# Eight transposes in a step, turned values, later loads, and blocks of unread 512-column products in an attention and feed-forward kernel

## The chip, the core and the metric

The kernel runs on one core of a Trainium2 chip. The metric is the device time of one execution in microseconds (us). The core's engines are named as the profile names them: PE (TensorE, the products; PEld is its weight load), DVE (VectorE), ACT (ScalarE), POOL (GpSimd) and SP (SyncE, which here only issues DMAs). They run side by side, each in its own order, and wait for each other by semaphores.

## The reference

Eight batches, eight heads, 512 local and 32 global tokens, 64 values a head. Attention comes first: global tokens look at everything, a local token looks at the global ones and at local ones no more than 32 away. Its output is the input of a feed-forward layer that mixes each token with the one before it. The core of both, cut:

```python
s_g = scale * np.matmul(q_g, k_all.transpose(0, 1, 3, 2))
out_g = np.matmul(sm(s_g), v_all)
s_ll = np.where(np.abs(pos[:, None] - pos[None, :]) <= 32, scale * (q_l @ k_l.T), -1e9)
out_l = np.matmul(sm(concat([s_lg, s_ll])), concat([v_g, v_l]))
...
xk = mu_k * x + (1.0 - mu_k) * x_prev
xr = mu_r * x + (1.0 - mu_r) * x_prev
k = np.maximum(xk @ w_k, 0.0)
v = k * k @ w_v
r = 1.0 / (1.0 + np.exp(-(xr @ w_r)))
return (r * v).astype(np.float32)
```

All is float32. `w_k` is 512 x 1024, `w_v` 1024 x 512, `w_r` 512 x 512.

## The kernel before, in words

A float32 product is made of three products of rounded parts (F32R): high by high, high by low, low by high (`products`, and `Keys.product` for the values). A tile of tokens has 256 columns, so nearly every product on PE is 128 x 128 by 256 columns, each with its own weight load.

A batch of the feed-forward layer has two tiles of 256 tokens. For each tile `keys` makes relu and square of xk @ w_k (four steps of 24 products), `gates` the gate from xr @ w_r (two steps of 24 products, each in a bank of its own, with a tanh on ACT behind each). From batch 2 (`FROM`) on, the two tiles' values are made together by seven products of sums instead of eight (`values_1`, three steps, and `values_2`, four, each of 24 products of 256 columns; in the trace they are `ps_m<-bh,a` and `ps_m<-bl,a`). The sums of `w_v` that they need lie in DRAM (`scratch`) and are loaded into `left`, five buffers of 512 KB, in the order of use; `load_left` issues the next loads when a product has let buffers go. The sums and differences of the squares (`part`, `difference`, `made`, `left_over`, on ACT, DVE and POOL) are made a few steps ahead, by the table `todo` in `batch`, whose numbers are steps of the batch.

The attention of batch b + 1 runs within batch b of the feed-forward layer. It goes by pairs of units (a unit is two heads of a batch). In `attention` a pair is seven steps: four groups of four transposes of the probabilities `Pt` (two units, two halves each; each group into a bank with the tag "t", from which ACT copies it into `PT`), two groups of three transposes for the global tokens (`Pg`), with the scores of the next pair behind the second, and the weighted sums. The probabilities are divided by their sums on POOL (`Pt<-Pt,ssum`, L413), queued in `softmaxes`. `in_turn` sets attention steps (A) and feed-forward steps (F) in turn by the strings in `BATCH`. Batch 7, the last, has no attention beside it: `batch(B - 1, last)` runs alone, and `end` does the values of batch 7 and the layer for all global tokens.

PE follows the order in which the code records its instructions (`in_line`); ACT, DVE and POOL follow it too (`by_hand`); SP's order is left to the scheduler outside the first part. PSUM has eight banks; `psum(tag)` takes the next of the pools that the current table gives a tag:

```python
MIDDLE_USE = {"m": [ps2, ps2, psx], "s": [ps4] * 4, "t": [ps1]}
LAST_USE = {"m": [ps2, ps2, psx, ps4, ps4, ps4, ps4]}
```

`fill(bank, n)` puts n transposes of the identity into a bank that is written over afterwards. Before the change, there are four of them in the last `gates` of batch 7, ahead of its second half.

`behind(store)` makes a DMA wait for the last square recorded on ACT (`Tokens.square`).

Of the kernel before, what the change touches and what calls it, by code (L numbers as in the profile page):

```python
# [10 lines left out]
F32 = mybir.dt.float32  # L11
# [5 lines left out]
AF = mybir.ActivationFunctionType  # L17
# [3 lines left out]
P = 128  # L21
# [69 lines left out]
def local_global_attention_then_rwkv_ffn(  # L91
# [44 lines left out]
    def change_use(to):  # L136
        nonlocal use
        use = to
        turn.clear()

    def psum(tag):
        n = turn[tag] = turn.get(tag, -1) + 1
        pool = use[tag][n % len(use[tag])]
        return pool.tile([P, 512], F32, tag="ps", name=f"ps_{tag}")
# [185 lines left out]
    to_load = [a for a, _ in V1 + V2] * (B - FROM) + ["A11", "A21", "A12", "A22"]  # L330
    left = []

    def load_left():
        if to_load:
            a = LEFT.index(to_load.pop(0))
            for i in range(0, HC, 2):
                part = leftp.tile([P, 2, 2, TOK], F32R, tag="a", name="a")
                nc.sync.dma_start(out=part.bitcast(F32), in_=scratch[:, a, i:i + 2])
                left.append(part)


# [87 lines left out]
    def pitched(j, h, g0, n):  # L429
        return PT[:, j, h, g0 * PITCH:(g0 + n) * PITCH].rearrange("p (g q) -> p g q", g=n)[:, :, 0:W]  # L430

    def transposes(r, h, j=None, n_fill=0):

        tp = psum("t")
        fill(tp, n_fill)
        for i in range(4):
            transpose(tp[:, i * P:(i + 1) * P], r.Pt[:, 4 * h + i], ident)

        def copy():
            if j is not None:  # L440
                nc.scalar.copy(pitched(j, h, 0, 4), tp.rearrange("p (g q) -> p g q", g=4))  # L441
            else:
                g0 = 2 * r.slots[0][1]
                out = PT[:, :, h, g0 * PITCH:(g0 + 2) * PITCH].rearrange("p j (g q) -> p j g q", g=2)[:, :, :, 0:W]
                nc.scalar.copy(out, tp.rearrange("p (j g q) -> p j g q", j=2, g=2))
        return copy
# [141 lines left out]
    def products(out, w_h, w_l, cols, x_h, x_l, n):  # L588
        for i in range(n):
            matmul(out, w_h[:, i, cols], x_h(i), start=(i == 0), stop=False)  # L590
            matmul(out, w_h[:, i, cols], x_l(i), start=False, stop=False)
            matmul(out, w_l[:, i, cols], x_h(i), start=False, stop=(i == n - 1))

    class Tokens:
# [72 lines left out]
        def squares(self, k2):  # L667

            for f0 in range(0, NF, 2):
                kp = psum("m").rearrange("p (j n) -> p j n", j=2)  # L670
                for j in range(2):
                    products(kp[:, j], wk_h, wk_l, slice((f0 + j) * P, (f0 + j + 1) * P),
                             lambda c: self.xk_h[:, c], lambda c: self.xk_l[:, c], NC)
                rk = self.two(tmpp, "relu")
                nc.scalar.activation(rk, kp, AF.Relu)  # L675
                nc.scalar.activation(k2[f0 // HC][f0 % HC // 2], rk, AF.Square)
                yield

        def gates(self, pool=None, n_fill=0):

            pool = pool or gatep
            self.gate = pool.tile([P, NC, TOK], F32, tag="gate", name="gate")
            for e0 in range(0, NC, 2):
                rp = psum("m").rearrange("p (j n) -> p j n", j=2)
                if e0:
                    fill(rp[:, 0], n_fill)
                for j in range(2):
                    products(rp[:, j], wr_h, wr_l, slice((e0 + j) * P, (e0 + j + 1) * P),
                             lambda c: self.xr_h[:, c], lambda c: self.xr_l[:, c], NC)
                nc.scalar.activation(self.gate[:, e0:e0 + 2], rp, AF.Tanh, scale=0.5)  # L690
                if e0 + 2 == NC:
                    nc.scalar.activation(self.gate, self.gate, AF.Copy, scale=0.5, bias=0.5)
                yield

        def values(self):
# [195 lines left out]
    def attention(pairs, R, Pg):  # L891

        for pair, nxt in zip(pairs, pairs[1:] + [None]):
            for s in nxt or ():
                load_qk(s)
            for j, r in enumerate(R):
                for h in range(2):
                    transposes(r, h, j)()
                    yield
            transposes_global(Pg, 0)()  # L900
            yield
            transposes_global(Pg, 1)()
            if nxt:
                R = [scores(whole(s)) for s in nxt]
                halves = list(product(R, range(2)))
                halves[0][0].exps(0)
                for (r, h), (r_next, h_next) in zip(halves, halves[1:]):
                    softmaxes.append((lambda r=r, h=h: r.norm(h), lambda r=r_next, h=h_next: r.exps(h)))
            yield
            if nxt:  # L910
                G = Global(nxt)
                G.make("s", "t")
                G.read()
                Pg = G.Pg
            weighted(pair, True)()
            if nxt:
                softmaxes.append((lambda: R[1].norm(1), G.exps))
                softmaxes.append((G.norm,))
            for s in nxt or ():
                load_v(s)  # L920
            yield pair[1].c + 1 == NC
# [55 lines left out]
    def fill(bank, n):  # L977
        for _ in range(n):
            transpose(bank[:, :P], ident, ident)
# [199 lines left out]
    def batch(b, before):  # L1179
# [28 lines left out]
        t0, t1 = this.tokens  # L1208

        def gates_of(n):  # L1210
            yield from this.tokens[n].gates(gate3 if (2 * b + n) % 3 == 2 else gatep, 4 * (b == B - 1 and n == 1))

        def begin_halves():
            nonlocal leftp, sump, gate3
# [11 lines left out]

        if b == FROM:
            steps = chain(before.values(), this.keys(t0), gates_of(0), this.keys(t1), gates_of(1))
            todo = {
                0: lambda: mix(t0, "r0"),  # L1230
                1: lambda: mix(t0, "r2"),
                3: lambda: begin_halves(),
                7: lambda: mix(t1, "k0"),
                8: lambda: (mix(t1, "k2"), this.part("B11", 0)),
                9: lambda: (mix(t1, "r0"), this.part("B11", 1)),
                10: lambda: (mix(t1, "r2"), this.difference("T1", 0)),
                11: lambda: (this.part("B21", 0), this.difference("T1", 1)),
                12: lambda: (this.part("B21", 1), this.made("T2", 0)),
                13: lambda: (this.difference("T2", 1), mix_next("k0")),
                14: lambda: mix_next("k2"),  # L1240
                15: lambda: (mix_next("r0"), this.difference("T3", 0)),
            }
        else:
            steps = chain(before.values_1(), this.keys(t0), gates_of(0), before.values_2(), this.keys(t1), gates_of(1))
            todo = {
                0: lambda: (before.left_over(0), mix(t0, "r2")),
                1: lambda: before.left_over(1),
                2: lambda: before.left_over(2),
                3: lambda: before.left_over(3),
                4: lambda: before.left_over(4),  # L1250
                6: lambda: mix(t1, "k0"),
                7: lambda: mix(t1, "k2"),
                8: lambda: mix(t1, "r0"),
                9: lambda: before.left_over(5),
                10: lambda: (before.left_over(6), mix(t1, "r2")),
                11: lambda: this.part("B11", 0),
                12: lambda: (this.part("B11", 1), this.part("B21", 0)),
                13: lambda: (this.part("B21", 1), this.difference("T1", 0)),
                14: lambda: this.difference("T1", 1),
                15: lambda: this.made("T2", 0),  # L1260
                16: lambda: (this.difference("T2", 1), mix_next("k0")),
                17: lambda: mix_next("k2"),
                18: lambda: (mix_next("r0"), this.difference("T3", 0)),
            }
        for n, _ in enumerate(steps):
            if b == FROM and n != 7:
                soften()
                softened = True
            todo.get(n, lambda: None)()
            if b == FROM and n in (8, 11):  # L1270
                load_left()
            yield

    def place(name, bufs):
# [5 lines left out]
    def keys_at(b):  # L1280
        if b not in keys_of:
            keys_of[b] = Keys(tokens_of(b))
        return keys_of[b]

    BATCH = {
        FROM - 1: "AFAFAFAFAF" "AFFAFFF" "AFAFAFAFAF" "AFFAFFF",
        FROM: "AFAFAFAFAF" "AFAF" "AFAFAFAFAF" "AFFAFF",
        None: "AFAFAFAFAF" "AFFAFF" "AFAFAFAFAF" "AFFFAFF",
    }
    last = first[1]  # L1290
    change_use(MIDDLE_USE)
    for b in range(1, B):
        if b < B - 1:
# [3 lines left out]
                pass  # L1297
            last = keys_at(b) if b >= FROM else batch.last
    t, = final.tokens
    for _ in batch(B - 1, last):  # L1300
        pass
    last = keys_of[B - 1]

    def end():
        change_use(LAST_USE)
        keys, gates = final.keys(t), t.gates()
        values, ends = chain(last.values_1(), last.values_2()), final.values_of_one()
        at, to = last.part, last.difference
# [69 lines left out]
```

## Time and profile before

| what | us |
|---|---|
| median of two runs | 639.13 (638.2 and 640.06) |
| the profiled execution | 637.5 |
| its span, first to last instruction | 635.6 |
| PE busy in the span | 621.7 |
| granted clock of PE | 1.000 of full speed |

A row of the page on engines has busy time, its share of the span and the number of instructions. In the chain of waits a row has the start and the length in us, and what ran or was waited for; "x24" counts the instructions merged in it. "issue" is time in which the engine waited for nothing that the profile shows. In the chain all products of the layer are `ps_m`, transposes of `Pt` and `Pg` are `ps_t L163`, scores and weighted sums are `ps_s`, and the filling transposes are `ps_m L163`. In a window's row stand the length, busy time and count of PE, PEld, DVE, ACT and POOL, the granted clock, the DMA share and GB/s. A mean duration of a product includes its way through the array, which overlaps with the next one.

Roughly, the first 100 us hold the loading and splitting of the weights and the first batches' attention; from there to about 514 us attention and layer run in turn; from 526 us on only the layer and the end of it.

### The profile page before, as it was taken

What the parts mean: (1) busy time and instruction counts of PE and PEld (TensorE: products, weight loads), DVE (VectorE), ACT (ScalarE), POOL (GpSimd) and SP (SyncE); (2) the same over time, 40 slices, a digit from 0 to 9 for tenths busy, and PEclk for the clock granted to TensorE, in tenths of its full rate; (3) what the DMA queues carried; (4) which work ended last, traced back from release to release, by engine and by line L of the source; (5) the groups of instructions that cost most, each with busy time, mean ns of one, the idle gap of its engine ahead of it and who ended that gap; (6) DMA issues with size and microseconds to landing.
All of it is one profiled execution on the core that took longest, in us unless ns stands there. A gap on an engine that the chain in (4) does not pass through costs nothing.

```text
span 635.6 us, 20448 instructions
## 1 busy us (share of the span) xinstructions
PE 621.7 (98%) x8355; PEld 595.7 (94%) x8355; DVE 440.5 (69%) x1238; ACT 382.8 (60%) x1154; POOL 336.8 (53%) x292
## 2 busy tenths in 40 slices
PE   6899999999999999999999999999999999999997
PEld 4688999999999899999999999999999999999997
DVE  7998983759888387676696677667686647465730
ACT  6898967164373678565847667575747654434431
POOL 3786455436855245846275535745375535551930
PEclk9999999999999999999999999999999999999999
DMA  8965562457395705658372756558371743271775
GB/s 334 378 214 194 212 224 86 166 197 269 104 326 167 299 3 215 201 197 293 128 263 86 286 193 229 186 200 313 128 262 54 235 173 119 98 264 53 249 232 182
DMA packets 43278, 127.29 MB, mean 200 GB/s; under 512 B 3760, under 2 KB 20656, under 8 KB 43184
## 3 DMA queue, kind: packets, MB, share of 16 engines
q1 hardware_dynamic: 43184, 125.98, 56.0%
q8 instruction: 66, 1.08, 0.7%
q14 instruction: 28, 0.23, 0.1%
HBM read 108.66 MB, written 17.30 MB: 198 GB/s over the span
## 4 chain that ended last, share of the span: by engine, by line
PE 81%; DVE 5%; DMA 3%; POOL 3%; issue 1%; ACT 1%; SPq 0%; DVEq 0%; POOLq 0%; ACTq 0%
PE ps_m L160 64%; PE ps_s L160 12%; PE ps_t L163 5%; DMA w<-w_v 1%; DMA raw_qk<-qk 1%; DMA a<-scratch 1%; POOL wk_l L271 1%; DVE a L299 1%; DVE diff L637 1%; POOL Pt L413 1%; POOL w L252 1%; PE ps_t L160 1%; DVE diff L632 0%; POOL wv_l L271 0%; DVE xfull L637 0%
## 5 line engine op out<-in xcount | busy, mean ns | idle before, releaser
L160 PE MATMUL ps_m<-xkh,wk_h 128*128 128x256 f32 x544 | 154.9, 285 | 0.1
L160 PE MATMUL ps_m<-xkl,wk_h 128*128 128x256 f32 x544 | 151.0, 277 | 0.0
L160 PE MATMUL ps_m<-xkh,wk_l 128*128 128x256 f32 x544 | 150.8, 277 | 0.0
L160 PE MATMUL ps_m<-bh,a 128*128 128x256 f32 x736 | 136.5, 282 | 0.2 <-DMA a<-scratch 0.2
L160 PEld LDWEIGHTS ps_m<-bh,a 128*128 128x128 f32 x736 | 114.7, 189 | 0.4 <-issue 0.4
L413 POOL TENSOR_TENSOR Pt<-Pt,ssum 128x512 f32<-128x512 f32 x64 | 69.4, 1088 | 83.3 <-ACT Pt L402 39.9
L402 ACT ACTIVATE Pt<-Pt,m 128x128 f32<-128x128 f32 x256 | 99.5, 396 | 12.6 <-DVE m L395 12.5
L160 PEld LDWEIGHTS ps_m<-xkh,wk_h 128*128 128x128 f32 x544 | 102.2, 188 | 3.9 <-issue 1.4
L160 PE MATMUL ps_m<-bl,a 128*128 128x256 f32 x368 | 102.7, 279 | 0.0
L160 PEld LDWEIGHTS ps_m<-xkl,wk_h 128*128 128x128 f32 x544 | 102.4, 188 | 0.1
L160 PEld LDWEIGHTS ps_m<-xkh,wk_l 128*128 128x128 f32 x544 | 102.3, 188 | 0.0
L642 POOL TENSOR_TENSOR xkl<-xfull,xkh 128x512 fp32r<-128x512 f32 x30 | 40.1, 1336 | 69.5 <-DVE ssum L359 43.8
L160 PE MATMUL ps_m<-xrh,wr_h 128*128 128x256 f32 x272 | 76.8, 283 | 0.0
L160 PE MATMUL ps_m<-xrl,wr_h 128*128 128x256 f32 x272 | 75.4, 277 | 0.0
L160 PE MATMUL ps_m<-xrh,wr_l 128*128 128x256 f32 x272 | 75.3, 277 | 0.0
L395 DVE CUSTOM_DVE_ANT_0 Pt<-ps_s,masks 128x128 f32<-128x128 f32 x256 | 55.8, 285 | 24.2 <-PE ps_s L160 24.2
L675 ACT ACTIVATE relu<-ps_m 128x512 f32<-128x512 f32 x52 | 30.9, 595 | 65.2 <-PE ps_m L160 65.1
L160 PEld LDWEIGHTS ps_m<-bl,a 128*128 128x128 f32 x368 | 69.2, 188 | 0.2 <-POOL bl L760 0.2
L441 ACT COPY PT<-ps_t 128x512 f32<-128x512 f32 x56 | 32.7, 584 | 52.5 <-PE ps_t L163 52.5
L642 POOL TENSOR_TENSOR xrl<-diff,xrh 128x512 fp32r<-128x512 f32 x30 | 41.3, 1376 | 40.2 <-DVE xrh L641 23.1
L637 DVE SCALAR_TENSOR_TENSOR diff<-diff,mu_r_sb,xT 128x256 f32<-128x256 f32 x56 | 58.1, 1076 | 0.0
L160 PEld LDWEIGHTS ps_s<-PT,raw_v 128*64 128x64 f32 x1568 | 50.0, 138 | 6.9 <-issue 3.1
(153 smaller groups left out, 1480.1 us busy)
## 6 DMA issues: line engine op xcount, KB each, us to landing
a<-scratch SPq DMA_DIRECT2D x92, 512.0 KB, 4.7
raw_v<-v SPq DMA_DIRECT2D x32, 896.0 KB, 7.3
raw_qk<-qk SPq DMA_DIRECT2D x32, 628.0 KB, 5.2
out_l<-gate SPq DMA_DIRECT2D x32, 256.0 KB, 4.0
w<-w_k SPq DMA_DIRECT2D x8, 512.0 KB, 12.1
w<-w_v SPq DMA_DIRECT2D x8, 512.0 KB, 3.7
w<-w_r SPq DMA_DIRECT2D x4, 512.0 KB, 4.1
scratch<-wv_h SPq DMA_DIRECT2D x8, 256.0 KB, 3.4
```

Of the source, the lines that this page charges most:

```text
L160: return in_line(nc.tensor.matmul(*a, **kw))
L163: return in_line(nc.tensor.transpose(*a, **kw))
L252: nc.gpsimd.tensor_scalar(word(n, F32, 1), word(n, F32, 1), REBIAS, 1.0, op0=ALU.mult, op1=ALU.mult)
L271: nc.gpsimd.tensor_sub(part_of_weights(n, "l"), word(n, F32, 0), part_of_weights(n, "h").bitcast(F32))
L299: nc.vector.tensor_sub(s.bitcast(F32R), s, hs.bitcast(F32))
L395: nc.vector.tensor_tensor_reduce(out=self.Pt[:, i], in0=self.place(t, n, h), in1=masks[:, 2 * self.slots[t][1] + n], op0=ALU.add, op1=ALU. ...
L402: nc.scalar.activation(self.Pt[:, i], self.Pt[:, i], AF.Exp, bias=self.low_x[:, i:i + 1], scale=-1.0, accum_out=self.ssum[:, i:i + 1],)
L413: nc.gpsimd.tensor_mul(self.Pt[:, some], self.Pt[:, some], inv.unsqueeze(2).to_broadcast([P, 4, W]))
L441: nc.scalar.copy(pitched(j, h, 0, 4), tp.rearrange("p (g q) -> p g q", g=4))
L637: nc.vector.scalar_tensor_tensor(self.shape(xf[:, j]), self.shape(d[:, j]), mu[:, c0 + j:c0 + j + 1], self.prev(c0 + j), op0=ALU.mult, op1 ...
L642: nc.gpsimd.tensor_sub(lo[:, both], xf, hi[:, both].bitcast(F32))
L675: nc.scalar.activation(rk, kp, AF.Relu)
```

## The change

Five things change.

- *Eight transposes in a step.* For pairs of batches above `FROM + 1` (batches 4 to 7: eight pairs, sixteen units), both halves of a unit are transposed in one step, the first into a bank "t", the second into a bank "s"; the two copies follow. A pair is then five steps, and `BATCH[None]` has two F between such steps.
- *A fill more.* `gates` takes the place of its fill from `FILL_AT`: as before in the last `gates` of batch 7, and now also in the last `gates` of batch 6, ahead of the second of the first step's two columns.
- *Values by turns.* In batch 7 the four steps of `values_2` and the four of the second tile's keys alternate, `todo` is moved accordingly, and `LAST_USE` holds from batch 7 on, not only in `end`.
- *Later loads.* Two loads of `left` in batch 2 wait for a square; `squares` now sets `Tokens.square`.
- *Unread products.* Where the fill is at (0, 2), that is in the last `gates` of batch 7, two further sets of `products` over two 256-column blocks at once (512 columns) are made into a bank that nobody reads. The block stands inside the loop over the two halves, so it is recorded twice.

```diff
-    def load_left():
+    def load_left(later=False):
...
-                nc.sync.dma_start(out=part.bitcast(F32), in_=scratch[:, a, i:i + 2])
+                load = nc.sync.dma_start(out=part.bitcast(F32), in_=scratch[:, a, i:i + 2])
+                if later:
+                    behind(load)
...
-    def transposes(r, h, j=None, n_fill=0):
+    def transposes(r, h, j=None, n_fill=0, bank="t"):
...
-                nc.scalar.activation(k2[f0 // HC][f0 % HC // 2], rk, AF.Square)
+                Tokens.square = nc.scalar.activation(k2[f0 // HC][f0 % HC // 2], rk, AF.Square)
...
             for e0 in range(0, NC, 2):
                 rp = psum("m").rearrange("p (j n) -> p j n", j=2)
-                if e0:
-                    fill(rp[:, 0], n_fill)
                 for j in range(2):
+                    if (j, e0) == fill_at:
+                        fill(rp[:, j], 4)
...
+                if (0, 2) == fill_at:
+                    wide = psum("m").rearrange("p (j n) -> p j n", j=2)
+                    for e in range(2):
+                        products(wide, wr_h, wr_l, slice(e * P, (e + 1) * P),
+                                 lambda c: self.xr_h[:, c // 2 * 2:c // 2 * 2 + 2],
+                                 lambda c: self.xr_l[:, c // 2 * 2:c // 2 * 2 + 2], NC)
                 yield
...
+            halves_of = [iter(range(2)) for _ in R]
             for j, r in enumerate(R):
-                for h in range(2):
-                    transposes(r, h, j)()
+                whole_unit = pair[0].b > FROM + 1
+                for copies in [["t", "s"]] if whole_unit else [["t"], ["t"]]:
+                    done = [transposes(r, next(halves_of[j]), j, bank=bank) for bank in copies]
+                    for copy in done:
+                        copy()
                     yield
...
+        if b == B - 1:
+            values, keys = before.values_2(), this.keys(t1)
+            by_turns = (x for pair in zip(values, keys) for x in pair)
+            steps = chain(before.values_1(), this.keys(t0), gates_of(0), by_turns, gates_of(1))
+            todo.update({
...
+    FILL_AT = {(B - 2, 1): (1, 0), (B - 1, 1): (0, 2)}
     BATCH = {
...
-        None: "AFAFAFAFAF" "AFFAFF" "AFAFAFAFAF" "AFFFAFF",
+        None: "AFFAFFAF" "AFFAFF" "AFFAFFAF" "AFFFAFF",
...
+    change_use(LAST_USE)
     for _ in batch(B - 1, last):
...
-        change_use(LAST_USE)
```

How the instructions stand. On PE, in the attention of batch 7, the end of a gate's products (`xrh`, `wr`), then a unit's transposes, then the first products of the values (`bh`, `bl`). Before:

```order
L160 MATMUL ps_m<-xrh,wr_l 128x256
L163 MATMUL ps_t<-ident,Pt 128x128 x4
L160 MATMUL ps_m<-bh,a 128x256
L160 MATMUL ps_m<-bl,a 128x256
L160 MATMUL ps_m<-bh,a 128x256 x2
```

Now:

```order
L160 MATMUL ps_m<-xrh,wr_l 128x256
L163 MATMUL ps_t<-ident,Pt 128x128 x4
L163 MATMUL ps_s<-ident,Pt 128x128 x4
L160 MATMUL ps_m<-bh,a 128x256
L160 MATMUL ps_m<-bl,a 128x256
L160 MATMUL ps_m<-bh,a 128x256 x2
```

The unit's second group, into `ps_s`, has moved up past the 24 products that stood between.

On PE, in the last `gates` of batch 7, between the first half and the second. Before:

```order
L160 MATMUL ps_m<-xrl,wr_h 128x256
L160 MATMUL ps_m<-xrh,wr_l 128x256
L163 MATMUL ps_m<-ident 128x128 x4
L160 MATMUL ps_m<-xrh,wr_h 128x256
L160 MATMUL ps_m<-xrl,wr_h 128x256
```

Now, at the end of the first block of wide products:

```order
L160 MATMUL ps_m<-xrl,wr_h 128x512
L160 MATMUL ps_m<-xrh,wr_l 128x512
L163 MATMUL ps_m<-ident 128x128 x4
L160 MATMUL ps_m<-xrh,wr_h 128x256
L160 MATMUL ps_m<-xrl,wr_h 128x256
```

24 wide products stand between the first half and the fill, and 24 more behind the second half, 48 rows of 128x512 in all.

On SP, in batch 2, the stores of the output and the loads of `left` (`a<-scratch`) against the next pair's loads (`raw_qk`, `raw_v`). Before:

```order
L882 DMA out_l<-gate 128x2x256
L338 DMA a<-scratch 128x1024 x3
L882 DMA out_l<-gate 128x2x256
L338 DMA a<-scratch 128x1024 x2
L349 DMA raw_qk<-qk 128x1256 x2
L354 DMA raw_v<-v 128x1792 x2
L349 DMA raw_qk<-qk 128x1256 x2
```

Now:

```order
L890 DMA out_l<-gate 128x2x256 x2
L351 DMA raw_qk<-qk 128x1256 x2
L356 DMA raw_v<-v 128x1792 x2
L338 DMA a<-scratch 128x1024 x5
L351 DMA raw_qk<-qk 128x1256 x2
```

The five loads of `left` have moved behind the pair's four.

More of the change, by code (lines that the diff above doesn't have):

```diff
@@ L430, in pitched @@
         return PT[:, j, h, g0 * PITCH:(g0 + n) * PITCH].rearrange("p (g q) -> p g q", g=n)[:, :, 0:W]
-    def transposes(r, h, j=None, n_fill=0):
-        tp = psum("t")
+    def transposes(r, h, j=None, n_fill=0, bank="t"):
+        tp = psum(bank)
         fill(tp, n_fill)
@@ L675, in squares, with gates @@
                 nc.scalar.activation(rk, kp, AF.Relu)
-                nc.scalar.activation(k2[f0 // HC][f0 % HC // 2], rk, AF.Square)
+                Tokens.square = nc.scalar.activation(k2[f0 // HC][f0 % HC // 2], rk, AF.Square)
                 yield
-        def gates(self, pool=None, n_fill=0):
+        def gates(self, pool=None, fill_at=None):
             pool = pool or gatep
@@ L1210, in gates_of @@
         def gates_of(n):
-            yield from this.tokens[n].gates(gate3 if (2 * b + n) % 3 == 2 else gatep, 4 * (b == B - 1 and n == 1))
+            yield from this.tokens[n].gates(gate3 if (2 * b + n) % 3 == 2 else gatep, FILL_AT.get((b, n)))
         def begin_halves():
@@ L1264, in batch @@
             }
+        if b == B - 1:
[3 more added lines that the diff above has]
+            todo.update({
+                10: lambda: mix(t1, "r2"),
+                11: lambda: before.left_over(6),
+                12: lambda: this.part("B11", 0),
+                13: lambda: (this.part("B11", 1), this.part("B21", 0)),
+                14: lambda: this.difference("T1", 0),
+                15: lambda: (this.part("B21", 1), this.difference("T1", 1)),
+                16: lambda: (this.made("T2", 0), mix_next("k0")),
+                17: lambda: (this.difference("T2", 1), mix_next("k2")),
+            })
         for n, _ in enumerate(steps):
@@ L1270, in batch @@
             if b == FROM and n in (8, 11):
-                load_left()
+                load_left(True)
             yield
```

## The prediction

> **What bounds the kernel.** I read the page from the top: busy times, the slices with the granted clock, then the chain of waits by engine.
>
> ```profile
> PE   621.7 (98%) x8355; PEld 595.7 (94%) x8355; DVE 440.5 (69%) x1238; ACT 382.8 (60%) x1154; POOL 336.8 (53%) x292
> ...
> PEclk9999999999999999999999999999999999999999
> ...
> PE 81%; DVE 5%; DMA 3%; POOL 3%; issue 1%; ACT 1%; SPq 0%; DVEq 0%; POOLq 0%; ACTq 0%
> ```
>
> The reader is to see that TensorE (PE) is busy nearly throughout, at full clock, and carries 81% of the chain; no other engine is near its limit. After the first 120 us nearly every microsecond on PE is a microsecond of the span. "Busy" hides one thing, though: records of products overlap, so it does not tell how fast they follow one another. The chain in order of time does: each row there is a stretch of PE with its count, and stretch over count is the spacing.
>
> ```profile
> 497.71 0.44 PE ps_t L163 x4
> 498.15 2.83 PE ps_m L160 x24
> 500.98 0.44 PE ps_t L163 x4
> 501.42 2.75 PE ps_m L160 x24
> 504.16 0.44 PE ps_t L163 x4
> 504.60 2.83 PE ps_m L160 x24
> 507.43 0.44 PE ps_t L163 x4
> 507.87 2.74 PE ps_m L160 x24
> ...
> 522.18 3.61 PE ps_s L160 x112
> 525.79 35.55 PE ps_m L160 x300
> 561.34 0.02 issue
> 561.35 5.68 DMA a<-scratch
> 567.03 0.14 issue
> 567.17 15.79 PE ps_m L160 x132
> 582.96 0.44 PE ps_m L163 x4
> 583.39 48.99 PE ps_m L160 x432
> 632.38 0.02 issue
> 632.40 0.42 DVE gate L711
> ```
>
> Two things stand here. First, from 498 us to 632 us PE never waits but for a DMA around 561 to 567 us. That row overstates it: 480 products at the 118 ns of that stretch fill 56.9 us of the 57.17 us from 525.79 to 582.96, so the wait costs about 0.3 us. Second, products of 256 columns follow one another at two spacings: 48.99 / 432 = 113.4 ns at the end, 35.55 / 300 = 118.5 ns before the four filling transposes at 582.96, and nothing in between; 24 products take 2.74 us or 2.83 us. After a group of four transposes the spacing is the other one: slow, fast, slow, fast. I call this the cadence. What sets it the trace does not tell; that four transposes turn it over is what these rows show, and the four fills at 582.96 do it too.
>
> **The change, part by part.** The sum is made against the profiled execution (637.5 us, span 635.6 us); it stands 1.6 us under the median of the runs, 639.13 us.
>
> *The wide products.* The words of the change say 24; the program has 48: the block stands inside the loop over the two halves of the gate, 24 behind each. Each reads 512 columns and has a weight load of its own. They stand on PE in the middle of the stretch above, where PE waits for nothing, so nothing covers them. No row has a product of this kind with 512 columns. The nearest are, from the timeline, plain float32 products,
>
> ```profile
> 30.84 1.89 PE L160 MATMUL ps_m<-xT,diag 128*128 128x256 f32 x8
> ```
>
> and, from the groups by shape, means of one instruction:
>
> ```profile
> L160 PE MATMUL ps_m<-xT,diag 128*128 128x256 f32 x32 | 7.8, 385 | 0.0
> L160 PEld LDWEIGHTS ps_m<-xrh,wr_h 128*128 128x128 f32 x272 | 51.0, 188 | 1.1
> ```
>
> The first shows eight plain float32 products of 256 columns: the last one's own 0.385 us off, seven spacings take 1.505 us, 215 ns each. The rounded products of the gate take 113 to 118 ns for the same width, about half. If the rounded product goes by columns, 512 of them take between 215 ns (twice the columns, each as in the fast half, with one fixed part) and 2 x 118.5 = 237 ns. Below that lies only the case in which the weight load sets the spacing: 118.5 ns, as now. Above it the case that the wide form goes at the plain rate, 2 x 215 = 430 ns. I take 220 ns, near the lower end of the inner pair, since twice the fast spacing is 226.8 ns and holds a fixed part twice: 48 x 0.220 = **+10.6 us** (inner ends +10.3 and +11.4; outer ends +5.7 and +20.6, kept as rivals). The banks they write are read by nobody, so ScalarE and VectorE get nothing to do, and the bank of each was last read seven tiles before.
>
> A rule to weigh here: the Trainium skill, "TensorE: Matmul & The Clock Gate", section "Back-to-back issue gap", gives about 131 ns for each product of 512 columns in a sustained stream of loads and products, and N / 2.4 + 2.5 ns, 216 ns, for one alone. By the first, 48 would cost 6.3 us as an estimate, by the second 10.4 us. No run here shows 512 rounded columns; what the trace shows, 113 ns at 256, leaves hardly 18 ns for the other 256 columns if the first held.
>
> *Eight transposes in a step.* For the pairs of batches 4 to 7, 16 units in all, two groups of four become one group of eight followed by 48 products. Before, a unit takes 0.44 + 2.83 + 0.44 + 2.75 = 6.46 us (rows from 497.71). After, it depends on the cadence behind eight. One earlier place shows it:
>
> ```profile
> 58.52 2.83 PE ps_m L160 x24
> 61.35 1.09 PE ps_s L160 x64
> 62.44 1.02 PE ps_t L163 x8
> 63.46 5.46 PE ps_m L160 x48
> ```
>
> Behind those eight the 48 products took 5.46 us, fast. If four turn the cadence over, eight leave it as it was, and it was fast before. So 0.87 + 5.46 = 6.33 us, 0.13 us less; with rounding I take 0.12 x 16 = **-1.9 us**. If eight leave it slow, 0.87 + 5.66 = 6.53 us, 0.08 us more a unit, +1.3 us. The second half of a unit is now wanted earlier. Its division on GpSimd is done in time:
>
> ```profile
> 460.25 1.22 POOL L413 TENSOR_TENSOR Pt<-Pt,ssum 128x512 f32<-128x512 f32 x1
> 464.34 1.22 POOL L413 TENSOR_TENSOR Pt<-Pt,ssum 128x512 f32<-128x512 f32 x1
> ```
>
> These are the last two divisions of the pair whose transposes began at 463.59 us by the chain; the last is done at 465.56 us, and the second group of eight would come at 463.59 + 6.33 = 469.9 us, 4.3 us later. The two copies of a unit now stand behind each other on ScalarE.
>
> ```profile
> L441 ACT COPY PT<-ps_t 128x512 f32<-128x512 f32 x56 | 32.7, 584 | 52.5 <-PE ps_t L163 52.5
> ```
>
> Two take 2 x 584 ns, and before most of them ScalarE had been waiting for PE (52.5 us in all); what is queued behind them there has a 2.7 us step more than before, so I cost it at nothing. If that cover were gone, the next group would wait by up to one copy, 0.6 us.
>
> *Fill, turns and banks at the end.* The fill behind the first 12 products of the stretch that begins at 525.79 adds 0.44 us and, as at 582.96, should turn slow to fast. Twelve at 118.5 ns, the fill, and 468 at 113.4 ns take 1.42 + 0.44 + 53.07 = 54.93 us against 57.17 us: **-2.2 us**. This holds the 0.3 us of the DMA wait, which goes because by turns each reader of `left` has 24 other products before the next (2.7 us more for its load). If the fill turns nothing, it costs 0.44 us, and the upper end is +0.4. Seven banks instead of three take no wait away, since no row above has one.
>
> *Later sums.* The five loads of `left` in batch 2 move behind the next pair's `raw_qk` and `raw_v` on the SP queue and behind a square on ScalarE.
>
> ```profile
> 203.78 2.94 PE ps_m L160 x24
> 206.72 0.26 PE ps_t L160 x3
> 206.97 0.81 issue
> 207.78 0.27 PE ps_t L160
> ```
>
> The same 4 us by engine, granted clock, DMA share and GB/s, and then what SP issued around them:
>
> ```profile
> 204.00:208.00 4.00, 3.19 (x30) 2.93 (x31) 2.67 (x26) 2.08 (x9) 1.04 (x1) 1.00 1.03 366
> ```
>
> ```profile
> 200.97 1.48 SPq L338 DMA_DIRECT2D a<-scratch  x3
> ...
> 208.93 0.82 SPq L349 DMA_DIRECT2D raw_qk<-qk  x2
> ```
>
> PE stands still for 0.81 us with nothing to wait for, while the DMA engines are full (share 1.03 in 204 to 208 us) with those loads. With the loads gone from there I take the stall as gone: **-0.8 us**, from 0 to about -1.5 us (two smaller stalls behind it may go too). They are read by the next batch's first `values`, from 250 us, so their lateness costs nothing; if they met the next `raw_qk` instead, the stall would come again there, at the same 0.8 us.
>
> *The cadence behind the wide block.* The last 432 products are fast now. Behind the second wide block nothing turns them over if they come out slow: 432 x (118.5 - 113.4) ns = 2.2 us. The rows leave it open: of the six stretches quoted from 498 us on three are slow. I take fast, since the fill just ahead of the last half of the gate and the block behind it bring the stretch out of a kind in which the loads have more time, which is a guess, and keep +2.2 for the range.
>
> Sum: 10.6 - 1.9 - 2.2 - 0.8 = +5.7 us: a span of 641.3 us, a profiled execution near 643.2 us, and from the median 639.13 + 5.7 = **644.8 us**.
>
> **The rivals.**
>
> (a) The wide block is paid in full, and the cadence does not come: eight transposes leave it slow, or the fill finds the stretch fast and turns it slow. For it: I know the turning only from four, and what stands before 525.79 is moved. 10.6 + 1.3 + 0.4 - 0.8 = +11.5, 650.6 us; with only some of it failing, 647 to 652.
>
> (b) The weight load sets the spacing: 48 x 0.1185 = 5.7, then -4.9 for the rest: 639.9 us. For it: every product has its own load of 188 ns, longer than the spacing of 113. Against it: plain products of twice the array time are spaced 215 ns with loads of the same size, so columns count.
>
> (c) The wide form goes at the plain rate: 48 x 0.430 = 20.6, -4.9: +15.7, 654.8 us. This ends on the other side. It decides from (12.8 + 4.9) / 48 = 0.37 us a product, 12.8 us being 2%. For it: plain float32 here takes twice as long per column. Against it: the operands are the same rounded tiles that take 113 ns for 256 columns, and only the width differs.
>
> (d) The change does what its words say, 24 products, not 48: 5.3 - 4.9, 639.5 us. Against it: both blocks stand in the program's order.
>
> **How the numbers follow.** A difference of 2% is about what a measurement of this kernel can tell from no change. Forecast (641.5 to 647): 0.56. Rival (a), 647 to 651.9: 0.27; its worst, with the last stretch slow too, passes 2%: 0.03. Rival (b): 0.05; by the page's rule it would be 639.13 + 6.3 - 4.9 = 640.5 us, in the same case. Rival (c): 0.06. Rival (d): 0.02. All gains at once with the wide block hidden, over 2% faster: 0.01. The range holds the forecast's bounds and (a): 641.5 (each inner bound at its best, 10.3 - 1.9 - 2.2 - 1.5 = +4.7, 643.8, less what two runs differ by, 1.9) to 651.5. Slower by over 2%: 0.06 + 0.03 = 0.09; faster 0.01; within 2% the rest, 0.90.
>
> **What would show it.** In the changed profile: 48 products 128x512 in two stretches of about 5.3 us each on the chain, PE busy throughout; at 215 to 227 ns the first step is right, near 119 (b), near 430 (c). Behind eight transposes a row of 48 at 5.46 us (right) or 5.66 us (wrong). Behind the new fill some 468 products at 113.4 ns without a row of DMA among them; 118.5 would make that step wrong. No issue row of 0.8 us near 207 us. The last stretch behind the second wide block at 113.4 ns. What would make the whole wrong is a new wait on PE, most likely for a copy behind eight transposes or for a split part in the turned order of the last batch.

## The result and the profile after

| | before | changed |
|---|---|---|
| median of two runs, us | 639.13 (638.2 to 640.06) | 648.11 (647.21 to 649.01) |
| ratio, 95% interval | | 1.0121 (1.0074 to 1.0168) |
| profiled execution, us | 637.5 | 649.01 |
| its span, us | 635.6 | 647.2 |

The changed kernel is 9.0 us slower by the medians; 644.8 was named, 641.5 to 651.5 was the range. The two profiles differ by more, 11.6 us of span. The chain of waits of the changed kernel in order of time, from the attention of batch 7 on:

```profile
500.36 0.44 PE ps_t L163 x4
500.80 0.44 PE ps_s L163 x4
501.24 5.46 PE ps_m L160 x48
...
524.59 3.61 PE ps_s L160 x112
528.21 1.61 PE ps_m L160 x12
529.82 0.44 PE ps_m L163 x4
530.25 58.65 PE ps_m L160 x492
588.90 0.44 PE ps_m L163 x4
589.34 54.60 PE ps_m L160 x456
643.93 0.03 issue
643.96 0.42 DVE gate L719
```

PE waits for nothing from 500 us to the end; the row of DMA that stood near 561 us is gone. The 492 products are 468 of 256 columns and 24 wide ones. At 113.4 ns the 468 take 53.07 us, which leaves 5.58 us for 24: 232.5 ns each. The 456 are 432, 48.99 us before, and 24 in 5.61 us. So 48 wide products cost 11.2 us, and the stretches around them run at the fast cadence.

Two landmarks split every run in three: the weighted sums near 240 us (a row of 116 products `ps_s`) and the last ones (112).

```profile
242.50 4.27 PE ps_s L160 x116
```

Before, that row began at 240.30 us. Up to it the changed kernel is 2.2 us late; between the landmarks it needs 282.09 us (before 281.88); behind the second 122.6 us (before 113.4). The last part is the change. The first is late although both kernels have the same order there up to about 200 us, and within 204 to 220 us the changed kernel even makes up 1.4 us. That is what the experiments had to sort out.

### The profile page after: what moved, and what is told of

Its sections match the earlier page's. It is cut to its first block, busy times and chain, and to the rows that moved or that the text cites. A ratio compares the mean times of both kernels' runs of the same rounds, so it can differ in the third digit from the quotient of the medians.

```text
span 647.2 us, 20580 instructions
## 1 busy us (share of the span) xinstructions
PE 631.6 (98%) x8407; PEld 603.0 (93%) x8407; DVE 439.5 (68%) x1238; ACT 382.7 (59%) x1154; POOL 335.9 (52%) x292
## 4 chain that ended last, share of the span: by engine, by line
PE 78%; DVE 7%; DMA 5%; POOL 3%; issue 1%; ACT 1%; DVEq 0%; POOLq 0%
PE ps_m L160 62%; PE ps_s L160 11%; PE ps_t L163 3%; DMA w<-w_v 3%; PE ps_s L163 1%; DMA raw_qk<-qk 1%; DMA raw_v<-v 1%; POOL wv_l L271 1%; DVE ps_s L260 1%; DVE ps_s L257 1%; DVE a L299 1%; DVE diff L639 1%; DVE Pt L397 1%; DVE w L263 1%; POOL w L252 1%
## 5 line engine op out<-in xcount | busy, mean ns | idle before, releaser
L160 PE MATMUL ps_m<-bh,a 128*128 128x256 f32 x736 | 131.3, 278 | 0.0
L160 PEld LDWEIGHTS ps_m<-bh,a 128*128 128x128 f32 x736 | 113.0, 188 | 0.0
L160 PE MATMUL ps_m<-xrh,wr_h 128*128 128x256 f32 (+1 forms) x288 | 83.1, 289 | 0.0
L160 PE MATMUL ps_m<-xrh,wr_l 128*128 128x256 f32 (+1 forms) x288 | 81.5, 283 | 0.0
L160 PE MATMUL ps_m<-xrl,wr_h 128*128 128x256 f32 (+1 forms) x288 | 81.5, 283 | 0.0
L768 DVE TENSOR_TENSOR bl<-B,bh 128x512 fp32r<-128x512 f32 x40 | 38.8, 985 | 27.6 <-ACT bh L767 27.1
L768 POOL TENSOR_TENSOR bl<-B,bh 128x512 fp32r<-128x512 f32 x36 | 48.9, 1378 | 16.6 <-ACT bh L767 10.9
```

The costliest lines, as they stand in the source:

```text
L160: return in_line(nc.tensor.matmul(*a, **kw))
L768: (nc.vector if b[0] == "B" else nc.gpsimd).tensor_sub(l, val, h.bitcast(F32))
```

## The experiments

The landmarks of all runs, in us of each one's profile, worked out from the chain's rows and the spans:

| run | start of the 116 | 116 to 112 | 112 to the end |
|---|---|---|---|
| before | 240.30 | 281.88 | 113.4 |
| changed | 242.50 | 282.09 | 122.6 |
| e1_again | 241.12 | 282.21 | 122.6 |
| e2_no_wide | 240.57 | 282.20 | 112.4 |
| e3_one_block | 240.55 | 281.47 | 117.0 |
| e4_wide_alone | 246.90 | 282.50 | 124.6 |
| e5_fill4 | 241.57 | 282.60 | 112.1 |
| e6_fill8 | 241.36 | 282.87 | 112.9 |
| e7_eight_alone | 242.03 | 282.44 | 113.4 |
| e8_later_alone | 241.03 | 283.21 | 113.0 |
| e9_widths | 240.37 | 282.38 | 120.5 |
| e10_narrow | 241.33 | 280.88 | 122.3 |
| e11_kept | 238.53 | 281.87 | 113.4 |
| e12_before | 242.24 | 281.76 | 113.0 |

### The two kernels once more

The changed kernel as it is:

> The changed kernel once more, to tell what belongs to it from what one execution shows. Theory 1 (columns): the only thing that costs is the wide block, 48 x 0.233 = 11.2 us; the 3.6 us by which the changed kernel's profile is already late at 195 us, where both kernels have the same order, is one execution's; then this profile's span is 642 to 645 us, the lateness at 195 us is another one, and the ratio to the kernel before is 1.010 (11.2 - 1.4 later loads - 1.2 eight transposes net - 2.3 fill and turns = +6.3). Rival (the early part is slower in this program): late again by 3 to 4 us at 195 us, span near 647 us, ratio 1.015 to 1.018.

Measured: 647.8 us against 640.02, ratio 1.0118 (1.0084 to 1.0153), span 645.9, and 2.2 us late at 195 us against the first profile of before, not 3.6 again. So the early lateness is not the program's, as theory 1 has it, though the span lies 0.9 us above its range. And the kernel before as it is:

> The kernel before itself, profiled once more, for the early part. Theory (the first profile of it was a lucky one): this profile is 1 to 4 us later at 195 us than the first, its span is 636 to 639 us, and the ratio is 1.000 within its interval. Rival (the change slows the early part): as quick at 195 us as the first profile, within 0.5 us.

Measured: ratio 0.9998 (0.9976 to 1.0019), span 637.0, and 1.8 us later at 195 us than its first profile. So the first profile of before was a quick one. The rows of the windows 14 to 24 and 24 to 30 us show where a part of it comes from (length, busy time and count of PE, PEld, DVE, ACT, POOL, then the granted clock). The first profile of before:

```profile
14.00:24.00 10.00, 7.13 (x169) 6.12 (x169) 9.56 (x36) 8.80 (x34) 6.31 (x8) 1.00 1.02 416
24.00:30.00 6.00, 4.69 (x82) 3.61 (x78) 5.71 (x23) 5.96 (x35) 4.84 (x6) 1.00 0.89 319
```

Its second profile:

```profile
14.00:24.00 10.00, 6.59 (x107) 5.22 (x107) 7.92 (x23) 6.79 (x26) 6.02 (x7) 0.83 1.02 415
```

The changed kernel's first:

```profile
24.00:30.00 6.00, 4.69 (x78) 4.07 (x75) 5.55 (x22) 5.97 (x34) 4.81 (x5) 0.80 0.82 296
```

The mean clock granted to PE was 0.80 to 0.83 in a window of the latter two and 1.00 in the first, and with it goes a lateness of 1.9 us by 28 us in the second profile of before. It comes and goes with the same kernel. It is not all: the changed kernel's first profile loses 1.7 us there, and more than that again between 60 us (1.2 us late) and 150 us (3.6 us late); no run tells why. e1_again and e12_before share the lower clock and are nearly alike at 195 us (2.2 and 1.8 us late), so they are the pair to compare: 645.9 - 637.0 = 8.9 us, of which -1.1 up to the first landmark, +0.45 between, +9.6 behind.

### The wide products

Without them:

```diff
-                if (0, 2) == fill_at:
-                    wide = psum("m").rearrange("p (j n) -> p j n", j=2)
...
```

> Leaves out the unread wide products, all else as in the changed kernel. Theory 1: 11.2 us less than the changed kernel, so about 5 us (0.8%) faster than the kernel before, ratio 0.990 to 0.994. Rival (the wide block is partly paid by waits that it hides): less than 9 us between the two, and new waits on the matrix engine behind the last batch's gates.

Measured: 637.37 us, ratio 0.9957 (0.9935 to 0.9978), so faster than both kernels. The last part is 10.1 us shorter than with them, between the theory's 11.2 and the rival's 9, and the new wait that the rival named is there. The chain shows what they had covered:

```profile
591.74 0.12 POOL xrl L644
591.87 1.41 issue
593.28 1.74 POOL bl L762
595.02 0.04 issue
```

Without the wide block a product waits for GpSimd's split of T2 (`bl`; 0.5 us by the waits of PE), and some of the products around it run at the slow cadence. With the block GpSimd has 11 us more, and the wait is gone: about 1 us of the block's 11.2 is paid by the wait and the slow products that it does away with.

One block, the one behind the second half:

```diff
-                if (0, 2) == fill_at:
+                if (0, 2) == fill_at and e0:
```

> One wide block of 24 in place of two, the one behind the second half. Theory 1: 5.6 us under the changed kernel, ratio to before 0.999 to 1.003. Rival (the first block hides a wait, or the second does): the two blocks are not worth the same, 3 us or 8 us instead of 5.6.

Measured: 641.78 us, ratio 1.0025 (1.0001 to 1.0048). The last part: 5.6 us less than with two, 4.6 us more than with none. The two are not worth the same, as the rival had it in kind: the block behind the second half covers the wait by itself, and the other one then costs its full 5.6 us. The first block alone was not run.

The kernel before with both blocks alone:

```diff
+                if n_fill:
+                    wide = psum("m").rearrange("p (j n) -> p j n", j=2)
...
```

> The kernel before with the two wide blocks alone. Theory 1: +11.2 us, ratio 1.0175, spacing of the wide products 225 to 236 ns as in the changed kernel, and no other row of the chain altered. Rival (spacing depends on the cadence in which the stretch ran before): another spacing than 233 ns, near 220 or 227, and +10.5 us.

Measured: 651.16 us, ratio 1.0166 (1.0129 to 1.0203); the profile is that of the slowest of the seven executions. The wide products are spaced 233 ns here too, where the stretch ahead of them ran at 118 ns; the rival's 220 or 227 did not come. From its row of 112, at 529.40 us, to the end it takes 124.6 us, 11.2 to 11.6 more than the kernel before. The end reads as in the changed kernel:

```profile
595.67 0.44 PE ps_m L163 x4
596.11 54.60 PE ps_m L160 x456
```

Why 233? Four widths in one kernel, 12 products each:

```diff
+                        n = (512, 448, 384, 320)[e0 + e]
...
+                        products(wide[:, :n], wr_h, wr_l, slice(e * P, (e + 1) * P),
```

> The unread products in four widths, 12 of each: 512 and 448 behind the first half of the gate, 384 and 320 behind the second; all else as in the changed kernel. Theory (a cost for each column at the slow cadence and no fixed part beside it, 0.45 ns a column from 118 ns at 256 to 233 at 512): 146, 175, 204 and 233 ns. Rival 1 (0.417 ns a column and 7 ns fixed, as the fast cadence of 256 suggests): 140, 167, 193 and 220 ns, and 512 alone is out of line. Rival 2 (the width 512 alone is dear, since a product fills its bank): 320 to 448 on rival 1's line.

The timeline has the first product of each width and what follows the last (start, length of one, engine, line, shapes):

```profile
581.30 0.39 PE L160 MATMUL ps_m<-xrh,wr_h 128*128 128x512 f32 x1
...
584.09 0.36 PE L160 MATMUL ps_m<-xrh,wr_h 128*128 128x448 f32 x1
...
586.52 0.60 PE L163 MATMUL ps_m<-ident 128*128 128x128 f32 x4
...
589.71 0.33 PE L160 MATMUL ps_m<-xrh,wr_h 128*128 128x384 f32 x1
...
591.78 0.31 PE L160 MATMUL ps_m<-xrh,wr_h 128*128 128x320 f32 x1
...
593.54 0.28 PE L160 MATMUL ps_m<-bh,a 128*128 128x256 f32 x1
```

Twelve of 512 take 2.79 us, of 448 2.43, of 384 2.07, of 320 1.76: 233, 203, 173 and 147 ns. That is 0.45 ns a column and some 3 ns beside it, and the line meets 118 ns at 256 columns, the slow cadence. Both rivals fall, by the trace of one execution (645.02 us). A second, faster spacing was seen at 256 columns alone: at 512 it was 233 ns behind fast stretches and behind the slow one of e4_wide_alone. The prediction's 220 ns was drawn from the fast one. What makes the line pass through the slow spacing stays open.

The same columns in 96 products of 256:

```diff
-                        products(wide, wr_h, wr_l, slice(e * P, (e + 1) * P),
+                        for y in range(2):
+                            products(wide[:, y], wr_h, wr_l, slice(e * P, (e + 1) * P),
```

> The same unread columns in 96 products of 256 columns in place of 48 of 512. Theory: 96 at 113.4 ns, 10.9 us, so 0.3 us less than the 11.2 us of the wide ones. Rival (the narrow ones pay for 48 loads more): over 11.2 us, by the slow cadence 11.3.

Measured in the chain:

```profile
527.43 0.44 PE ps_m L163 x4
527.87 58.50 PE ps_m L160 x516
586.36 0.44 PE ps_m L163 x4
586.80 54.43 PE ps_m L160 x480
```

480 products at 113.4 ns. 58.50 us is 0.15 us less and 54.43 us 0.17 us less than the stretches with wide products: 0.3 us, as expected (one execution, 646.28 us). The wide form saves 48 loads and is still the dearer one.

### The cadence

The new fill alone in the kernel before:

```diff
+                    if n_fill < 0 and (j, e0) == (1, 0):
+                        fill(rp[:, j], -n_fill)
```

> The kernel before with the new fill of four transposes alone, behind the first 12 products of batch 6's last gates. Theory (the cadence is the reason): the 480 products behind the last weighted sums take 1.6 + 0.44 + 53.1 us, plus 0.3 us of DMA wait, 55.4 instead of 57.2, so 1.8 us less in that stretch and nothing altered elsewhere; by time 0.3% faster, ratio 0.995 to 1.000. Rival (the fill matters only together with the turned values or the seven banks): the stretch stays at 118 ns a product and gets 0.44 us longer.

Measured: 638.38 us, ratio 0.9992 (0.9967 to 1.0017). The chain:

```profile
527.78 1.61 PE ps_m L160 x12
529.39 0.44 PE ps_m L163 x4
529.83 53.76 PE ps_m L160 x468
```

1.61 + 0.44 + 53.76 = 55.81 us instead of 57.17: 1.4 us less. By its starts the stretch runs at 113.3 ns up to the place of the DMA wait, near 567 us; there two spacings of 146 and 195 ns stand, and behind them it runs at 117.8 ns to its end. A short wait turned the cadence.

Eight in place of four:

> The same place, eight transposes instead of four. Theory 1 (four turn the cadence over, so eight leave it as it was): the products behind stay at 118 ns, the stretch takes 57.2 + 0.9 = 58.1 us. Rival (any fill lets the stretch begin anew, and it begins fast): 113.4 ns behind it, 1.6 + 0.87 + 53.1 + 0.3 = 55.8 us.

```profile
527.84 1.61 PE ps_m L160 x12
529.46 0.87 PE ps_m L163 x8
530.33 32.68 PE ps_m L160 x288
```

288 products in 32.68 us, 113.5 ns: fast behind eight as behind four. (639.6 us, ratio 1.0006, 0.9983 to 1.003; the DMA wait, a hold-up of 0.4 us by the starts, again turned the rest slow.) So the fill does not turn the cadence over. Whatever its number, the stretch behind it began fast, in the kernel before and in the changed one, from slow and from fast.

Counted by starts over all fourteen profiles from 100 us on, the stretch behind a fill was fast in all 18 cases, 14 of them out of a slow one. Behind four transposes of `Pt` the cadence was the other one in 398 of 414 cases. Behind eight it was the same as ahead of them in all 128: fast in 126, slow in two (e11_kept, near 391 and 398 us).

### Eight transposes in a step, alone

```diff
-                for h in range(2):
-                    transposes(r, h, j)()
-                    yield
+                for copies in [["t", "s"]] if whole_unit else [["t"], ["t"]]:
+                    done = [transposes(r, next(halves_of[j]), j, bank=bank) for bank in copies]
...
```

> The kernel before with eight transposes in a step alone. Theory: sixteen units of 6.34 us instead of 6.46, 1.9 us less; four stretches of 48 behind the scores turn slow, 4 x 0.2 us more; and one or two stalls of about 0.5 to 1.2 us without a releaser near 303 and 377 us, as in every run with this part so far, so the gain is nearly given back: between -1.2 and +0.6 us from 246 us to the weighted sums near 522 us. Rival (the stalls come from the later loads, which move the loads of left): no stall without a releaser behind 246 us here, and 1.1 us less.

Measured: 639.82 us, ratio 1.0027 (1.0001 to 1.0054). Between the landmarks it needs 282.44 us, about what the kernel before needs (281.88 and 281.76). Its units run at 0.88 + 5.46 us, but the chain has

```profile
304.18 1.01 PE ps_m L160 x7
305.19 1.07 issue
306.26 2.79 PE ps_m L160 x23
```

and 0.83 us more of the same near 379 us. In e12_before PE runs through this place:

```profile
304.94 4.17 PE ps_m L160 x35
```

The later loads are not in e7_eight_alone, so they are not the only reason, and the rival falls. But a stall at the first place is not bound to the eight transposes either: e8_later_alone, which has none, shows 0.72 us there, and e6_fill8, which has neither part, 0.37 us. Over the profiles of the table, the six without this part need 281.8 to 283.2 us between the landmarks, 282.5 in the mean, the eight with it 280.9 to 282.4, 281.9 in the mean: 0.5 us are left of 1.9.

The starts say where the rest went. At the fast cadence throughout and with no hold-up, every one of the fourteen profiles would need 279.4 to 279.6 us between the landmarks. Slow stretches add 2.0 to 2.7 us without the part and 0.4 to 1.2 with it, 1.3 us less in the mean. Hold-ups of PE add 0.3 to 1.5 us without it and 1.1 to 2.3 with it, 1.0 us more. The four slow stretches of 48 that the expectation names are three here (5.85 us instead of 5.66) and four in e1_again, but four also in e4_wide_alone, which lacks the part, and none in e10_narrow, which has it.

### Later loads, alone

```diff
-                load_left()
+                load_left(True)
```

> The kernel before with the later loads alone. Theory: the stall of 0.8 to 1.1 us without a releaser near 207 us is gone and the stretch from 200 to 222 us is 1.4 us shorter, ratio 0.996 to 1.000. Rival (it comes again later, where the loads go now): the gain at 222 us is lost by 250 us, or stalls without a releaser come at about 303 and 377 us.

Measured: 638.03 us, ratio 0.9975 (0.995 to 1.0). In e12_before the chain has, where the loads of `left` fill the DMA engines,

```profile
208.54 0.26 PE ps_t L160 x3
208.80 1.25 issue
```

and e8_later_alone has no such row; between 202 and 221 us it makes up 1.5 us against the first profile of before (2.2 us late, then 0.7), and the gain is still there at 253 us. The first half of the rival falls. The second half holds in part: the stall at 305 us, 0.72 us, came here too.

The traces also tell what PE stands still for, though the chain names no releaser. The list of DMA queues on the page (packets, MB, share) has, for the kernel before and for the changed one,

```profile
q8 instruction: 66, 1.08, 0.7%
```

that is packets of 16 KB, one for each 256 of PE's 16889 instructions in the trace of before (products, weight loads and the sequencer's); e10_narrow, with the most instructions, has 67. In all fourteen profiles together there are 21 rows of "issue" of 0.25 us or more between 200 and 524 us. Each stands right ahead of one of the same three of PE's instructions, which lie 11 and 8 blocks of 256 apart, and each ends 1.2 to 1.5 us behind the landing of that block's packet. Of some 900 blocks in all profiles none begins sooner than 1.2 us behind its packet. The reading that fits all of this is that PE waits there for its own instructions, whose packet comes late while loads fill the DMA engines. Ahead of the stall near 304 us the packet started 1.6 to 1.8 us after the block before it had begun in e1_again, e7_eight_alone and e8_later_alone, and 0.1 and 0.9 us after it in the two profiles of before. No run moved the packets by themselves.

### What could be kept

The changed kernel without the wide products, without the fill in the last gates of batch 7, and with the last mixing of r for the global tokens behind the split of T2:

```diff
...
+                18: lambda: this.difference("T3", 0),
...
-    FILL_AT = {(B - 2, 1): (1, 0), (B - 1, 1): (0, 2)}
+    FILL_AT = {(B - 2, 1): (1, 0)}
...
-            lambda: (at("T2", 1), to("T4", 0)),
+            lambda: (at("T2", 1), to("T4", 0), t.mixing("r0")),
```

> The changed kernel without the unread products, without the fill in the last gates of batch 7 (the stretch is fast there already), and with the mixing of the last r of the global tokens behind the split of the sum T2, so that GpSimd gets the split first. Theory: the wait of 0.46 us for GpSimd's split that the kernel without the wide products shows near 594 us is gone, the tail from the last weighted sums to the end is 111.4 us (112.5 - 0.44 - 0.6), and it beats the kernel before by 0.5 to 0.7%, ratio 0.993 to 0.996. Rival (the fill is needed): without the four fills the products behind go at 118 ns, 2 us more, and the ratio is 0.997 to 0.999.

Measured: 636.27 us, ratio 0.9962 (0.9946 to 0.9978). It beats both kernels, but not e2_no_wide by anything that can be told. The last part did not get shorter (113.4 us):

```profile
584.98 1.91 issue
586.89 0.02 POOLq L762
586.90 0.02 issue
586.92 1.67 POOL xkl L644
588.59 0.04 issue
588.64 11.46 PE ps_m L160 x95
```

PE now waits 0.6 us for another piece of GpSimd's work, the low part of the mixed k. By its starts it runs at 113.4 ns before that wait and for 60 products behind it; two small hold-ups follow, near 596 and 598 us (0.3 us together), and from there it runs at 117.8 ns to the end. The wait was moved, not removed, and the slow cadence is what the rival foretold, though not for its reason: the stretch was fast without the fill, and the hold-ups turned it.

## Why the prediction was right, and where not

The time lies in the range, 3.3 us over the number named, and by its place in the band given to rival (a). Rival (a) is not what happened: eight transposes and the fill were both followed by the fast cadence. Without the room for it the range would have ended at 647, so that the range held the time is in part luck. The terms of the sum were right in kind, and three of them were mis-sized instead. Step by step, against the pair e1_again and e12_before:

- *The wide products, +10.6.* 48 of them stand on the chain, uncovered: right in kind. 233 ns each and not 220: +11.2 us. The step that failed is the choice near the lower end, "since twice the fast spacing is 226.8 ns and holds a fixed part twice". Some 3 ns of fixed part show between 320 and 512 columns, and the spacing lies above twice the fast one. The inner ends, 215 and 237 ns, held it. Rivals (b), (c) and (d) are out: 119 and 430 ns were not seen, and 48 ran. The Trainium skill ("TensorE: Matmul & The Clock Gate", section "Back-to-back issue gap") gives about 131 ns for 512 columns in a sustained stream of loads and products; the trace does not agree, with 233 ns.
- *Eight transposes, -1.9.* The units run as said, 0.88 + 5.46 us, and for the reason given: eight left the cadence as it was. What was not foreseen is that PE stalls without a releaser near 304 and 378 us: 1.22 and 0.28 us in e1_again, none over 0.2 us there in the two profiles of before.

```profile
304.26 1.22 issue
...
378.15 0.28 issue
```

Nor was it foreseen that the four stretches of 48 behind the scores are slow in e1_again and fast in both profiles of before, 0.8 us in all. That step, "I cost it at nothing" for all but the transposes themselves, gave the rest back: +0.45 us between the landmarks of the pair, and -0.5 in the mean of all profiles. The copies, the banks and the division on GpSimd, where a wait was feared, cost nothing: in the changed kernel and in e1_again the two stalls are PE's only waits from 246 to 524 us.

- *Fill, turns and banks, -2.2.* By starts, from the first of the 12 to the first wide product, 12 + 4 + 468 took 55.0 us (54.9 were named), against 57.1 us in the first profile of before. Against e12_before, whose 480 products took 56.6 us by starts without a DMA wait, it is 1.6 us.

```profile
527.61 56.73 PE ps_m L160 x480
```

The size was right against the first profile, and the reason half wrong. That the fill turns the cadence over falls with e6_fill8; that it came out fast at the new place agrees with all other fills. And removing the DMA wait is worth more than its 0.3 us (0.44 us by the starts): alone, the fill gave 1.4 us, since the hold-up left there turns the last 132 products slow. No run has the turned values or the seven banks alone.

- *Later sums, -0.8.* The stall near 207 us is gone, in all eight profiles that have the part. With a shorter wait near 213 us that goes too, it is 1.5 us by e8_later_alone, the far end of what was allowed for.
- *The cadence behind the wide block.* Fast, as taken, though by a guess, as the prediction says.

Summed for the pair: +11.2 for the wide products, -1.6 for the rest of the last part, +0.45 between the landmarks, -1.1 ahead of them, 8.9 us. Against the 5.7 us named that is 0.6 more for the wide products, 2.3 for the eight transposes and what came with them, 0.6 for the fill, and 0.3 less ahead. Two slips in the prediction change nothing: the slow spacing is 117.8 ns by starts and not 118.5, and the working of the lower bound gives 641.9 and not 641.5.

What stays open: what sets the cadence (behind four transposes of `Pt` it was nearly always the other one, behind eight the same, behind a fill always fast; no run tells why), and why PE's packet near 304 and 378 us comes later with eight transposes. The stalls there stand where the DMA engines are full or have just been, as the stall near 207 us does. The row of e1_again ahead of its larger stall, with the DMA share as the last number but one:

```profile
300.00:303.00 3.00, 3.00 (x140) 2.80 (x138) 1.12 (x2) 2.00 (x4) 0.35 (x1) 1.00 1.03 349
```

That loads cause the stall was shown by an experiment for 207 us alone, by moving them.

## What to carry to other kernels

Where one engine fills the chain, price added work by start-to-start spacing at its own width, not by a mean duration (396 ns for a wide product that costs 233) and not by doubling a narrow one. Read a regular stretch twice, for its waits and for its spacing: here 4 ns a product over 480 products were worth more than the one visible wait, and a hold-up of 0.1 to 0.4 us (e5_fill4, e6_fill8) cost another 0.6 us by the slower spacing of the 132 products behind it. Where an engine stands still with nothing to wait for, look at the instruction queue among the DMA queues. And profile the unchanged kernel more than once before a sum is made against it: between two profiles of it, 1.8 us were gone before the changed code was reached.

## What the runs showed of the hardware that was not expected

- Rounded products with a load each, 128 x 128 weights: 113.4 or 117.8 ns at 256 columns, never a steady value between, then 147, 173, 203 and 233 ns at 320, 384, 448 and 512.
- With nothing to stop PE the cadence lasts: 480 products at 117.8 ns (e12_before), over 500 at 113.4 ns (e10_narrow). A hold-up of PE turned it from fast to slow (0.1 us in e5_fill4, 0.4 us in e6_fill8), from slow to fast (0.5 us near 569 us in e8_later_alone, 0.7 us near 594 us in e2_no_wide), or left it (0.4 us, slow, near 567 us in the first profile of before; 0.8 us, fast, near 588 us in e11_kept).
- No block of 256 instructions of PE began sooner than 1.2 us behind the landing of its 16 KB packet on queue q8, and where the packet came late PE stood still for up to 1.25 us.
- The granted clock of PE was 0.66 to 0.83 in a window of 6 to 10 us between 14 and 30 us in all profiles but two (the first of before and e11_kept, the two with the earliest first landmark). In the clock records of the traces these are stretches of 3.41 us, or of twice that (e10_narrow, e4_wide_alone), at 0.5 of full speed. One profile (e4_wide_alone), with 0.61 from 30 to 36 us as well, was over 6 us late by 195 us.

```profile
30.00:36.00 6.00, 6.00 (x31) 3.94 (x30) 2.61 (x6) 2.99 (x15) 5.15 (x6) 0.61 0.70 286
```
